# Half-shifted frequencies in a blocked FFT convolution, with shifted filter spectra formed by an add and the taps of the shift convolution summed by accumulating transfers

## The chip, the cores and the metric

The kernel runs on one core of a Trainium2 chip. The metric is the time of one execution on the device in microseconds (us). The core has five engines with a queue of instructions each: PE (TensorE, matrix products into PSUM), DVE (VectorE, elementwise work), ACT (ScalarE, elementwise work and PSUM evictions), POOL (GpSimd, which also issues transfers) and SP (SyncE, which only issues transfers and waits). The engines meet through semaphores.

## The reference

The input is one sequence of S = 2048 rows and D = 640 channels, in bfloat16. Two layers follow each other, each behind a layer norm (LN): a gated long convolution, and a feed-forward network (FFN).

```python
k_shift = sum over t < 4 of k_pad[:, t:t+S, :] * shift_k[:, 3-t]     # 4 taps per channel
kv = k_shift * v
y  = irfft(rfft(kv padded to 2S) * rfft(ssm_k padded to 2S))[:S]      # causal convolution, per channel
y  = y + kv * ssm_D
h  = x + layernorm(x) * y
h2 = h + (silu(layernorm(h) @ w_gate) * (layernorm(h) @ w_up)) @ w_down
```

The FFN's weights are 640 x 1728 (gate, up) and 1728 x 640 (down).

## The kernel before

**Blocks.** The sequence is cut into four blocks of B = 512 rows, j = 0 to 3, and the channels into two halves of CW = 320, c = 0 and 1. The long convolution is computed blockwise. Block i of kv has a spectrum X_i, lag m of the filter has a spectrum K_m, each of a transform of N = 1024 points, and the output of block j is the inverse transform of the sum of X_i K_(j-i). A filter spectrum of lag m covers two neighbouring blocks of the filter, m and m - 1, since a window of 1024 points is needed for an output of 512.

**A transform.** Rows are laid out as four interleaved groups b of 128 rows, so that a transform has two stages with a shuffle between them. In `fwd` (line 704), stage 1 multiplies each group by two 128 x 128 tables; in a K transform of j > 0 it accumulates two sources, the block's filter rows with the table `oS1` and the previous block's with a second table, `oS1A` (line 1100), whose entries carry the sign of the frequency's parity. The result is evicted, and four transfers from SBUF to SBUF regroup the partitions (the shuffle). Stage 2, `stage2` and `spec` (lines 779 and 794), multiplies by 128 x 64 tables, T = 0 and 1 in two halves of PE's columns. h = 0 to 3 numbers the four groups of frequencies, `hs` is a pair of them.

**Frequency 0.** Frequencies are whole numbers, and so 0 and N/2, whose spectra are real, share a row of real and imaginary parts. For that row the product's cross terms differ. K therefore has an extra piece for h = 0 (the cells named "d"): two more matmuls and an eviction of 320 columns in `spec`, four matmuls and an eviction in `dense_h` (line 735), and the second product of h = 0 stands apart from that of the other h (lines 833 to 842).

**Products and inverse.** `products` (line 818) multiplies spectra on DVE: for each term one product of real with real and imaginary with imaginary parts, one of the crossed parts, and adds into two accumulators. `combine` (line 859) forms the real and the imaginary part. For j = 2 the two accumulators aren't combined, and `inv2` (line 869) takes four operands instead of two; for j = 3 the terms of X_1 K_2 and X_2 K_1, summed earlier into the place of X_1, are brought in as two further operands. After `inv2` come an eviction with a scale, a shuffle back (`rs`), and the last stage in `conv_bp` (line 1067), with the gate by the normed x, the residual sum, and the LN's statistics. Block 0 takes a short way: `dense_c` (line 750) multiplies by dense tables of the whole transform, which are loaded at the start in nine pieces (`den_piece`).

**The taps.** `kv_block` (line 976) makes kv: on DVE, a product of the loaded rows of k by each of four taps (t0 and t1 take turns as targets), three adds into t0, and a product with v.

```python
mul(t0, 0); mul(t1, 1); add(); mul(t1, 2); add(); mul(t1, 3); add()
vec(... vt = vt * t0 ...)
```

**Buffers.** Tiles come from pools with few slots, given out in a fixed order. A load into a slot waits until the slot's last reader is done: KIN (rows of k) and VIN (rows of v) have one slot, TMP (t0, t1) two, KT (the filter's rows) three, TX (forward and inverse stages) three, EP (normed rows and gated outputs) four. For most blocks the filter is transposed by a transfer, stored to the scratch tensor `k_nat` and loaded again (`load_kraw`).

**Order.** `Prog.schedule` (line 130) writes every engine's queue out before the kernel runs: it steps through time with a cost for each operation and a model of the transfers (`dma_model`, line 1249), and gives each free engine the ready operation of highest priority. Convolutions go ahead of FFN work, whose matmuls fill the gaps. `pe_end` models the clock of PE. `emit` (line 237) turns the order into instructions with semaphore waits; an instruction whose wait isn't satisfied holds everything behind it on its engine. At the end SP waits for every semaphore that a transfer has used (line 305, `tail`, line 336). Loads for j > 0 and the FFN weights are issued from POOL, the shuffles, the output's stores and the filter's transposes from SP. The `pow` of each LN is also POOL's (line 934).

The functions that the change touches, with the line numbers of the profile:

Of the kernel before, what the change touches and what calls it, by code (L numbers as in the profile page):

```python
# [40 lines left out]
class Prog:  # L41
# [5 lines left out]
    def __init__(self):  # L47
        self.ops, self.pools = [], {}

    def pool(self, name, bases, inorder=False):  # L50
        self.pools[name] = Pool(bases, inorder)

# [55 lines left out]
    def pe_end(self, t, c):  # L108

        w = self.clock  # L110
        while c > 1e-12:
            k = int((t + 1.7) // self.WIN)
# [124 lines left out]
    def emit(self, nc, es, block, ndma_sems):  # L237
# [67 lines left out]
        tail = [(s[0], s[1]) for s in dsem if s[1]]  # L305
# [33 lines left out]
def _tables(R):  # L339
    N = 256 * R  # L340
    B = N // 2
# [3 lines left out]
    s1a = np.zeros((128, 2, 128))  # L345
    for T in range(2):
        f1 = (64 * T + np.arange(64))[None, :]
        s1f[:, T, 0:64] = np.cos(2 * np.pi * q * f1 / 256)
        s1f[:, T, 64:128] = -np.sin(2 * np.pi * q * f1 / 256)
        sg = np.where(f1 % 2 == 0, 1.0, -1.0)  # L350
        s1a[:, T, 0:64] = s1f[:, T, 0:64] * sg
        s1a[:, T, 64:128] = s1f[:, T, 64:128] * sg
    s1f[:, 0, 64] = (-1.0) ** np.arange(128)
    s1a[:, 0, 64] = (-1.0) ** np.arange(128)
    s1i = np.stack([s1f[:, T, :].T for T in range(2)], axis=1)
    w2 = np.zeros((2, R, 128, 2, 64))
    wk = np.zeros((128, 2, 64))
    w2i = np.zeros((128, R, 2, 128))
    for T in range(2):
        for G in range(R):  # L360
            for i in range(I1):
                f1 = 64 * T + R * i + G
                for m in range(R):
                    col = i * R + m
                    for b in range(R):
                        r0, r1 = i * R + b, 64 + i * R + b
                        if f1 == 0:
                            if m == 0:
                                w2[T, G, r0, 0, col] = 1.0
                                w2[T, G, r0, 1, col] = (-1.0) ** b  # L370
                                continue
                            f, r = (256 * m, r0) if m < R // 2 else (128 + 256 * (m - R // 2), r1)
                            th = 2 * np.pi * b * f / N
                            w2[T, G, r, 0, col] = np.cos(th)
                            w2[T, G, r, 1, col] = -np.sin(th)
                            continue
# [7 lines left out]
    wk[:, 0, :] = w2[0, 0, :, 1, :]  # L384
    wk[:, 0, 0] = 0.0
    wk[:, 1, :] = w2[0, 0, :, 0, :]
    wk[:, 1, 0] = w2[0, 0, :, 1, 0]
    w2i[0, 0, :, :] *= 0.5
    w2s = np.transpose(w2, (2, 0, 1, 3, 4)).reshape(128, -1)
    w2in = -w2i[:, :, 0, :]  # L390
    cols = [s1f.reshape(128, -1), s1a.reshape(128, -1), s1i.reshape(128, -1), w2s, wk.reshape(128, -1),
            w2i.reshape(128, -1), w2in.reshape(128, -1), np.eye(128)]
# [7 lines left out]
def _dense_tables(R):  # L400
# [5 lines left out]
    kx = np.zeros((2, R, 128, 128))  # L406
    iv = np.zeros((R, 2, R, 128, 128))
    for h in range(R):
        for T in range(2):
            for i in range(I1):  # L410
                f1 = 64 * T + R * i + h
                for m in range(R):
                    row = T * 64 + i * R + m
                    if f1 == 0 and m == 0:
                        c, s = np.ones_like(t) * 1.0, (-1.0) ** t
                        wc, ws = 0.5 * c, 0.5 * s
                    else:
                        f = f1 + 256 * m
                        if f1 == 0:
                            f = 256 * m if m < R // 2 else 128 + 256 * (m - R // 2)  # L420
                        c = np.cos(2 * np.pi * f * t / N)
                        s = -np.sin(2 * np.pi * f * t / N)
                        wc, ws = c, s
                    fw[h, 0, :, :, row], fw[h, 1, :, :, row] = c, s
                    iv[h, 0, :, row, :], iv[h, 1, :, row, :] = wc, ws
    kx[0], kx[1] = fw[0, 1], fw[0, 0]
    kx[0, :, :, 0] = 0.0
    kx[1, :, :, 0] = fw[0, 1, :, :, 0]
# [4 lines left out]
    return np.concatenate([lay(fw), lay(kx), lay(iv)], axis=1).astype(np.float16)  # L433


def bass_sequential_preLN__ssm_conv_h3__swiglu_ffn__prompt_kernel(
# [12 lines left out]
    CMB = [True, True, False, True]  # L449
    RESPE = [True, True, False, False]  # L450
    KDMA = [[False, False], [True, True], [True, True], [True, True]]
    S2M = False
    I2M = False
# [4 lines left out]
    tab_np, (oS1, oS1A, oS1I, oW2, oWK, oW2I, oW2N, oID) = _tables(R)  # L458
# [8 lines left out]
    with ExitStack() as es:  # L467
        NEL = 101900
# [50 lines left out]
        DROW = fix("drow", D)  # L519
# [5 lines left out]
        HNT = fix("hnt", 5 * 512)  # L525
        WROW = P.tile("wrow", None, HNT.base)
# [7 lines left out]
        P.pool("KT", slots(3, 4 * CW), True)  # L534
# [3 lines left out]
        skb, sk = slots(2, 9 * CW), slots(2, 9 * CW)  # L538
# [9 lines left out]
        P.pool("EK", slots(1, 5 * CW), True)  # L548
        P.pool("PP", slots(3, 4 * CW), True)
        P.pool("P0", [HNT.base + i * 2 * CW for i in range(4)], True)  # L550
        P.pool("EP", slots(4, 2 * CW), True)
# [31 lines left out]
        def dma(subs, kb, reads, writes, prio, eng="sp", after=(), name="", shuffle=False):  # L583
            fns = [(lambda g, d=d, s=s: g.dma_start(d(), s())) for d, s in subs]  # L584
            return P.op({eng: (0.9 if eng == "pool" else 0.5) * len(subs)}, fns, reads, writes, prio, after=after, dma=(kb, shuffle), name=name)
# [39 lines left out]
        def load_kv(j, c, prio):  # L625
# [12 lines left out]
            if j == 0:  # L638
                P.op({"pool": 0.3}, lambda g: g.memset(V(kt, 0, 3 * CW, 0, 1), 0.0), [], [(kt, "z")], prio, name="kz")
# [4 lines left out]
            dma(subs, 573, [], [(kt, 0)], prio, name=f"kin{j}{c}", eng="pool" if j else "sp")  # L644
# [3 lines left out]
        def load_kraw(j, c, prio):  # L648
            if KDMA[j][c]:
# [6 lines left out]
                    [], [(t, 0)], prio, dma=(328 * 3, False), name=f"kraw{j}{c}")  # L656
# [17 lines left out]
        def k_natural(j, c, prio):  # L674
# [18 lines left out]
            pe(fns, 128, 25, [(kr, 0), (IDN, 0)], [(pt, 0)], prio, reserve=[(kt, 0)], name=f"ktr{j}{c}")  # L693
# [10 lines left out]
        def fwd(nm, srcs, pool, prio):  # L704
# [13 lines left out]
            for G in range(R):  # L718
                def src(G=G):
# [3 lines left out]
                    name=f"sh{nm}G{G}", shuffle=True)  # L723
# [5 lines left out]
        def oKX(i, b):  # L729
            return (8 * R + i * R + b) * 128  # L730
# [564 lines left out]
```

## Time and profile before

| | us |
|---|---|
| two executions | 330.1 and 331.59, median 330.85 |
| span of the profiled execution, first to last instruction | 324.5 |
| what the two executions have outside such a span | 5.6 and 7.1 |
| PE busy | 289.4 (89%) |
| DVE busy | 239.2 (74%) |
| ACT busy | 189.7 (58%) |
| POOL busy | 41.6 (13%) |
| transfers | 41.09 MB |

The profile gives the span of the execution that it shows, but not that execution's own time, which is one like the two in the first row. A busy time is the time in which an engine has an instruction in work. The groups of instructions give the mean of one instruction; since instructions overlap in an engine's pipeline, a full stream of them can run faster than the mean tells. Lines are often those of a helper: L593 is any matmul, L816 any operation of two tensors on DVE, L576 any eviction, L584 any transfer.

### The profile page before, as it was taken

The page shows a single profiled execution, that of the slowest core. Times are in us where ns is not written, and L with a number is a line of the kernel's source. Part 1 is how long each engine was busy: PE and PEld are TensorE (multiplying, and loading weights), DVE is VectorE, ACT ScalarE, POOL GpSimd, SP SyncE. Part 2 cuts the span into 40 slices and gives each one's busy share as a digit, 9 for nine tenths or more (in the row PEclk, how much of TensorE's full clock was granted, in tenths as well). Part 3 has the DMA queues.
Part 4 walks back from the last instruction along what each step waited for, and adds up shares of the span by engine and source line. Part 5 has one row for each costly group of instructions (what it writes and reads, how often), then busy time and mean ns, then how long its engine had stood idle before and what let it go on. Part 6 is the DMA issues. An engine that isn't in the chain of part 4 may idle for free. (4 is left out here: it accounts for less than half of the span.)

```text
span 324.5 us, 5040 instructions
## 1 busy us (share of the span) xinstructions
PE 289.4 (89%) x1853; PEld 157.9 (49%) x1872; DVE 239.2 (74%) x416; ACT 189.7 (58%) x304; POOL 41.6 (13%) x55
## 2 busy tenths in 40 slices
PE   4999773589989999998998999789999999999992
PEld 1567451334435466653443566444444576444571
DVE  1988959799899899799999998964598383332221
ACT  4488969767666758577847476679954412222100
POOL 2413125524010003010020000200100010000000
PEclk9999998589999999999999999959999999999999
DMA  7999979879862423424300224241201111000010
GB/s 203 361 403 217 250 232 296 265 210 289 265 194 90 134 103 68 169 91 154 121 2 21 101 63 152 81 154 42 81 0 42 40 41 42 0 2 0 0 53 31
DMA packets 33245, 41.09 MB, mean 127 GB/s; under 512 B 10488, under 2 KB 28307, under 8 KB 33220
## 3 DMA queue, kind: packets, MB, share of 16 engines
q1 hardware_dynamic: 29076, 26.06, 25.8%
q0 software_dynamic: 3296, 14.01, 14.4%
q10 hardware_dynamic: 848, 0.69, 0.8%
q8 instruction: 15, 0.25, 0.3%
q14 instruction: 10, 0.08, 0.1%
HBM read 22.40 MB, written 4.59 MB: 83 GB/s over the span
## 5 line engine op out<-in xcount | busy, mean ns | idle before, releaser
L593 PE MATMUL ps<-sb 128*128 128x320 bf16 (+2 forms) x1193 | 223.6, 339 | 6.4 <-DMA sb<-in_A_shift_k_dram 2.4
L816 DVE TENSOR_TENSOR sb<-sb 128x1280 bf16<-128x1280 bf16 (+2 forms) x266 | 168.8, 677 | 22.6 <-DMA sb<-in_A_k_dram 9.1
L593 PEld LDWEIGHTS ps<-sb 128*128 128x128 bf16 (+2 forms) x1212 | 116.0, 99 | 97.8 <-issue 12.3
L576 ACT ACTIVATE sb<-ps 128x640 bf16<-128x640 f32 (+2 forms) x139 | 94.3, 716 | 39.3 <-PE ps L593 33.5
L816 DVE TENSOR_TENSOR sb<-ps,sb 128x1024 bf16<-128x1024 f32 (+3 forms) x52 | 50.5, 982 | 46.3 <-PE ps L593 42.6
L593 PE MATMUL ps<-sb,tab 128*64 128x320 bf16 (+2 forms) x556 | 69.6, 316 | 13.8 <-ACT sb L576 5.6
L593 PEld LDWEIGHTS ps<-sb,tab 128*64 128x64 f16 (+2 forms) x556 | 34.1, 104 | 49.7 <-issue 21.2
L1165 ACT ACTIVATE sb<-ps 128x1024 bf16<-128x1024 f32 (+2 forms) x32 | 29.3, 915 | 42.1 <-PE ps L593 41.9
L944 ACT ACTIVATE sb<-sb,stt 128x320 bf16<-128x320 bf16 (+1 forms) x43 | 28.7, 722 | 16.5 <-DVE stt L936 12.9
L934 POOL TENSOR_TENSOR stt<-stt 128x2 f32<-128x2 f32 (+1 forms) x12 | 13.8, 1152 | 112.1 <-DVE stt L972 65.3
L579 ACT ACTIVATE sb<-ps 128x640 bf16<-128x640 f32 x24 | 16.0, 702 | 10.5 <-PE ps L593 10.4
L918 DVE BATCH_NORM_STATS2 stt<-sb 128x6 f32<-128x320 bf16 x32 | 13.7, 478 | 0.0
L963 ACT ACTIVATE sb<-sb,stt 128x640 bf16<-128x640 bf16 x16 | 13.2, 827 | 0.3
L1125 PE MATMUL ps<-sb 128*128 128x128 bf16 x80 | 6.8, 249 | 6.4 <-ACT sb L576 3.6
L584 POOL DMA_DIRECT2D sb<-in_A_v_dram x6 | 4.7, 777 | 59.7 <-PE ps L593 56.9
L956 ACT ACTIVATE sb<-sb 128x640 bf16<-128x640 bf16 x16 | 11.9, 742 | 0.0
L1125 PEld LDWEIGHTS ps<-sb 128*128 128x128 bf16 x80 | 5.8, 112 | 7.7 <-ACT sb L576 4.6
L584 POOL DMA_DIRECT2D sb<-in_A_k_dram x6 | 6.0, 995 | 19.7 <-DVE sb L816 19.6
L690 PE MATMUL ps<-sb 128*128 128x128 bf16 (+1 forms) x24 | 4.1, 283 | 2.2 <-DMA sb<-in_A_ssm_k_dram 2.2
L936 DVE TENSOR_TENSOR stt<-stt 128x2 f32<-128x2 f32 (+1 forms) x12 | 1.9, 160 | 5.6 <-POOL stt L934 5.5
L584 POOL DMA_DIRECT2D sb<-in_B_w_down_dram x6 | 4.3, 721 | 11.1 <-DMA sb<-in_B_w_down_dram 7.2
L584 POOL DMA_DIRECT2D sb<-in_B_w_gate_dram x6 | 3.6, 606 | 8.5 <-DMA sb<-in_B_w_gate_dram 7.8
(25 smaller groups left out, 35.3 us busy)
## 6 DMA issues: line engine op xcount, KB each, us to landing
sb<-sb SPq DMA_DIRECT2D x72, 160.0 KB, 2.2
sb<-in_A_k_dram POOLq DMA_DIRECT2D x6, 560.0 KB, 6.5
out_dram<-sb SPq DMA_DIRECT2D x16, 160.0 KB, 1.8
sb<-cst_den SPq DMA_DIRECT2D x9, 256.0 KB, 5.8
sb<-in_B_w_gate_dram POOLq DMA_DIRECT2D x5, 416.0 KB, 5.4
sb<-in_B_w_up_dram POOLq DMA_DIRECT2D x5, 416.0 KB, 6.0
sb<-in_A_q_dram POOLq DMA_DIRECT2D x3, 640.0 KB, 5.5
sb<-in_A_v_dram POOLq DMA_DIRECT2D x6, 320.0 KB, 4.4
```

The source lines that it names most:

```text
L576: fns = {"act": lambda a: a.activation(out=dst(), in_=src(), func=ACTF.Copy), "dve": lambda v: v.tensor_copy(out=dst(), in_=src())}
L579: fns = {"act": lambda a: a.activation(out=dst(), in_=src(), func=ACTF.Copy, scale=scale), "dve": lambda v: v.tensor_scalar(out=dst(), in0 ...
L584: fns = [(lambda g, d=d, s=s: g.dma_start(d(), s())) for d, s in subs]
L593: return lambda t: t.matmul(o(), l(), r(), start=st, stop=sp)
L816: return lambda v: v.tensor_tensor(out=o(), in0=a(), in1=b_(), op=op)
L918: vec(dve1(CW, False), lambda v: v.bn_stats(st6(l, j, b, c), V(xt, b * D + c * CW, CW)), [(xt, (b, c))], [(ST, ("s", l, j, b, c))], prio, ...
L934: P.op({"pool": 0.4}, lambda g: g.tensor_tensor(out=y, in0=va, in1=stt[:, 420:420 + hi - lo], op=ALU.pow), c1 + [(ST, "half")], c3, prio, ...
L944: "act": lambda a: a.activation(out=dst(), in_=src(), func=ACTF.Identity, scale=rs(l, j, b), bias=tmv(l, j, 3)[:, b:b + 1])},
L956: P.op({"act": act_c(D) + 0.22}, lambda a, b=b, jt=jt: a.activation(out=V(jt, 0, D), in_=V(xt, b * D, D), func=ACTF.Copy, accum_out=tmv(l, ...
L963: P.op({"act": act_c(D) + 0.3}, lambda a, b=b, jt=jt: a.activation(out=V(jt, 0, D), in_=V(xt, b * D, D), func=ACTF.Square, bias=tmv(l, j, ...
L1125: fns.append(lambda t, k=k, d=d: t.transpose(B16(pt, k, d * 128, 128), V(hn[k], d * 128, 128), V(IDN, 0, 128)))
L1165: P.op({"act": act_c(n)}, lambda a: a.activation(out=dst(), in_=src(), func=ACTF.Silu), rd, wr, -1000, name=f"si{j}{i}")
```

## The change

1. **Odd frequencies.** All frequencies are shifted by a half: f1 becomes f1 + 0.5 in all tables. No spectrum is real then, and the extra piece for frequency 0, its tables, matmuls, evictions and the split product go. The tables get smaller: the dense ones from 9 x 1024 to 8 x 1024 columns, the small one from 3584 to 2688.
2. **Shifted spectra by an add.** Stage 1 of K takes one source only. The spectrum of the block's own filter rows goes to a new tile SS (a pool of five slots), and `shift_add` makes the filter spectrum of the lag from it and the previous block's: two DVE operations of 640 elements per partition for each pair of h. KT falls to two slots.
3. **Two operands in every inverse.** For j = 2 the accumulators are combined too, and for j = 3 the earlier sums are added on DVE (`cx`, two operations for each pair of h) instead of in `inv2`.
4. **Tap sums by transfers.** For j > 0 the three adds of `kv_block` become three transfers from SBUF to SBUF that add to t0, issued from POOL. The product with the fourth tap is written over the k rows.
5. **Smaller things.** The gated output takes the place of the normed tile (EP falls to three slots). At the end SP waits for the semaphores of the output's last stores only. DROW lies in GUT. The costs and the model of transfers in the scheduler change, and with them the order that it writes.

```diff
-        tail = [(s[0], s[1]) for s in dsem if s[1]]
+        last = {}
+        for o in self.ops:
+            if o.dma is not None and not o.succ and o.name.startswith("st"):
+                last[id(o.sem)] = (o.sem, max(o.semval, last.get(id(o.sem), (None, 0))[1]))
+        tail = list(last.values())
...
-        f1 = (64 * T + np.arange(64))[None, :]
+        f1 = (64 * T + np.arange(64))[None, :] + 0.5
...
-    return np.concatenate([lay(fw), lay(kx), lay(iv)], axis=1).astype(np.float16)
+    return np.concatenate([lay(fw), lay(iv)], axis=1).astype(np.float16)
...
-        P.pool("KT", slots(3, 4 * CW), True)
+        P.pool("KT", slots(2, 4 * CW), True)
...
+        P.pool("SS", slots(5, 4 * CW), True)
...
-        P.pool("EP", slots(4, 2 * CW), True)
+        P.pool("EP", slots(3, 2 * CW), True)
...
+        def shift_add(dst, do, cur_, co, prv, po, hs, prio, nm):
+            rd = [(t, h) for t in (cur_, prv) for h in hs]
+            wr = [(dst, h) for h in hs]
+            o1 = vec(dve2(640), tt(lambda: V2(dst, do, 960, 2, CW), lambda: V2(cur_, co, 960, 2, CW), lambda: V2(prv, po + CW, CW, 2, CW), ALU.subtract),
+                     rd, [(dst, (h, "a")) for h in hs], prio, name=f"ks{nm}")
+            vec(dve2(640), tt(lambda: V2(dst, do + CW, CW, 2, CW), lambda: V2(cur_, co + CW, CW, 2, CW), lambda: V2(prv, po, 960, 2, CW), ALU.add),
+                rd + [(dst, (h, "a")) for h in hs], wr, prio, name=f"kp{nm}")
...
+            def acc(src, off, cells):
+                P.op({"pool": 1.0}, [lambda g: g.dma_start(V(t0, 0, W4), V(src, off, W4), accum_op=ALU.add)],
+                     [(t0, 0)] + cells, [(t0, 0)], prio, dma=(656, "acc"), name=f"kvd{j}{c}")
+
             mul(t0, 0)
             mul(t1, 1)
...
+            else:
+                acc(t1, 0, [(t1, 0)])
+                mul(t1, 2)
+                vec(dve2(W4), tt(lambda: v4(kt), lambda: v4(kt), lambda: tapb(3), ALU.mult),
+                    [(kt, 0), (kt, "z"), (TAPS, 3)], [(kt, 0)], prio, name=f"kvm{j}{c}")
+                acc(kt, 0, [(kt, 0)])
+                acc(t1, 0, [(t1, 0)])
...
-            if CMB[j]:
+            if j < 3:
                 combine(...)
+            else:
+                ax = SXt[1, c]
+                combine(...)
+                for a, o_ in ((a1, 0), (a2, CW)):
+                    vec(dve2(640), tt(lambda a=a: V2(a, 0, 640, n, CW), lambda a=a: V2(a, 0, 640, n, CW), lambda o_=o_: V2(ax, h0 * 640 + o_, 640, n, CW), ALU.add), ...,
+                        name=f"cx{nm}{h0}")
...
-            srcs = [(kts[j, c], oS1)] + ([(kts[j - 1, c], oS1A)] if j else [])
-            uk = fwd(f"K{j}{c}", srcs, "TK", pb + 104)
+            uk = fwd(f"K{j}{c}", [(kts[j, c], oS1)], "TK", pb + 104)
...
-            for hs in ([[0], [1], [2], [3]] if j == 0 else [[0, 1], [2, 3]]):
+            for hs in ([0, 1], [2, 3]):
...
-        link = [1.4]
+        link, turn = [2.6], [0.0]
...
-                    [], [(t, 0)], prio, dma=(328 * 3, False), name=f"kraw{j}{c}")
+                    [], [(t, 0)], prio, dma=(328, "turn"), name=f"kraw{j}{c}")
...
+            if kind == "shuffle":
+                s = max(issued, dmafree[0])
+                dmafree[0] = s + 0.3
+                return s + 1.65 + (1.6 if link[0] > issued else 0.0)
+            if kind == "store":
+                return issued + 1.3
+            if kind == "turn":
+                s = max(issued, link[0] + 1.0 if link[0] > issued + 2.0 else 0.0, turn[0])
+                turn[0] = s + 4.9
+                return turn[0]
+            s = max(issued + (1.3 if o.eng == "pool" else 0.9), link[0])
+            link[0] = s + kb / 345.0
+            return link[0] + 1.0
```

## The prediction, made before the change was run

> **What bounds it now.** First the page's first and second parts, for who is busy and when.
>
> ```profile
> span 324.5 us, 5040 instructions
> ...
> PE 289.4 (89%) x1853; PEld 157.9 (49%) x1872; DVE 239.2 (74%) x416; ACT 189.7 (58%) x304; POOL 41.6 (13%) x55
> ...
> PE   4999773589989999998998999789999999999992
> ...
> DVE  1988959799899899799999998964598383332221
> ...
> PEclk9999998589999999999999999959999999999999
> DMA  7999979879862423424300224241201111000010
> ```
>
> PE is the fullest, but DVE stands at 9 until slice 26. So I cut the span where its character changes: the table of windows (stretch, length; busy us of PE, PEld, DVE, ACT, POOL; clock; DMA share; GB/s).
>
> ```profile
> 52.00:58.00 6.00, 2.07 (x14) 0.86 (x14) 4.69 (x16) 6.00 (x12) 5.05 (x5) 0.65 1.07 335
> ...
> 64.00:124.00 60.00, 56.71 (x343) 27.13 (x348) 56.00 (x91) 41.23 (x62) 7.95 (x11) 0.97 0.59 178
> 124.00:182.00 58.00, 54.45 (x358) 28.31 (x360) 54.20 (x86) 40.22 (x65) 6.13 (x6) 1.00 0.27 90
> 182.00:207.00 25.00, 24.90 (x198) 16.34 (x200) 23.69 (x46) 13.87 (x23) 1.52 (x2) 1.00 0.28 99
> ...
> 213.00:268.00 55.00, 54.24 (x339) 27.91 (x344) 36.89 (x67) 32.64 (x56) 2.44 (x3) 0.96 0.14 53
> ```
>
> To 64 us transfers and short dependences leave PE idle; 64 to 207 has PE and DVE both at 93 to 100%; from 213 PE alone is full. Next, the groups by shape, for prices (count | busy us, mean ns | idle).
>
> ```profile
> L816 DVE TENSOR_TENSOR sb<-sb 128x1280 bf16<-128x1280 bf16 x158 | 127.2, 826 | 17.6 <-DMA sb<-in_A_k_dram 9.1 <-PE ps L593 4.1 <-DMA sb<-in_A_v_dram 1.8
> ...
> L816 DVE TENSOR_TENSOR sb<-sb 128x640 bf16<-128x640 bf16 x92 | 42.2, 483 | 5.0 <-PE ps L593 3.1 <-ACT sb L576 1.3
> ...
> L593 PE MATMUL ps<-sb,tab 128*128 128x320 bf16 x192 | 32.6, 299 | 5.4 <-DMA sb<-k_nat 3.1 <-ACT sb L576 2.2
> ...
> L593 PE MATMUL ps<-sb,tab 64*128 64x320 bf16 x160 | 14.5, 315 | 3.1 <-DVE sb L816 3.1
> ```
>
> Last the chain of waits (start, length, what), one row of the timeline, the tail line's row, and the landing of the output tensor's stores:
>
> ```profile
> 182.10 25.20 PE ps L593 x198
> ...
> 269.50 3.80 PE ps L593 x28
> ...
> 302.83 15.40 PE ps L593 x112
> ```
> ```profile
> 42.13 1.26 PE L593 MATMUL ps<-sb,tab 128*128 128x320 bf16 x8 [3.08 <-DMA sb<-k_nat]
> ```
> ```profile
> L336 SPq EVENT_SEMAPHORE  x69: 17/28/28, 319.6 to 324.1; - x69
> ```
> ```profile
> DMA to landing us min/median/max: 1.8/1.8/5.6
> ```
>
> The third piece gives 15.40/112 = 0.1375 us per 320-column matmul in a full stream; the timeline row shows PE standing 3.08 us for one transfer; the tail row shows 69 final waits, the last at 324.1.
>
> **The change, part by part.**
>
> *PE.* Stage 1 of K loses its second source: 8 matmuls in each of 6 blocks (j = 1 to 3, c = 0, 1), 48 x 0.1375 = 6.6 us. `inv2` goes from four operands to two for j = 2 and 3: 64 of the 160 half-height matmuls, which run two at a time, 32 x 0.1375 = 4.4. The extra spectrum of frequency 0 goes: 8 dense matmuls, 1.1, and 12 half-width ones in pairs, 0.8. Together 12.9 us of 289.4. ACT also loses 8 evictions of 320 columns (437 ns each); ACT isn't the limit.
>
> *DVE.* Gone: 18 adds of 1280 (three in each of six blocks), 18 x 0.826 = 14.9. Eighteen pairs of 640 products become one of 1280: 18 x (2 x 0.483 - 0.826) = 2.5. New, all 640: 24 in `shift_add`, 8 in `combine` for j = 2, 8 `cx` for j = 3: 40 x 0.483 = 19.3. Net +1.9 us. But it moves: in 64 to 207, 24 new (11.6), against 15 adds (12.4) and 14 merges (2.0): -2.8.
>
> *Tail.* SP waits only for the semaphores of the last stores, at most 16. The last store is issued at 319.2 and lands 1.8 later, at 321.0; the end at 324.1 is the list of waits, paid in full. Gain 3.0; bounds 2.5 (sixteen waits of 28 ns may follow the landing) and 3.1.
>
> *Start.* The dense tables shrink from nine pieces of 256 KB to eight, the small table from 896 to 672 KB: 480 KB, at the 282 to 372 GB/s of 10 to 30 us 1.3 to 1.7 us of a link whose share is 1. The dense stage loses 1.1 us of PE. The transfer models change too, so the order does: now PE waits 3.1 us at 39 to 42 for `k_nat` in front of dense work that was ready. The new model gives the transpose 4.9 us, which may move that stage-1 matmul back. Bounds 0 and 1.7 + 3.1 = 4.8; I take 3.1, about two thirds, since the link and this stall are in the chain to the first FFN at 64.
>
> *64 to 207.* PE sheds 8 x 0.1375 for each of K11, K20, K21, K30 (4.4), 2.2 in `inv2` of j = 2, 0.6 in the frequency-0 matmuls: 7.2. DVE sheds 2.8. Where both are full the smaller cut decides; the last 25.2 us, by the chain, are PE's own. So 2.0 (most of DVE's 2.8, up to 182) + 2.0 (PE's share after it: K31 or K30, half an `inv2`) = 4.0; bounds 0 and 7.2. The EP pool falls from four slots to three, so in the LN wait at 207 the fourth normalised tile waits for a transpose of 0.7 us: 0.7 back; bounds 0 and 0.7 at each of four LNs, 2.8.
>
> *207 to the end.* Of j = 3's PE work 2.2 (K stage 1) + 2.2 + 0.3 = 4.7 goes. What covers j = 3's convolution is FFN 2; its LN transposes run at 268.2 with one `dn` of 28 matmuls, 3.8 us, left in reserve. The cover shrinks by 4.7, the chain grows by four 640 operations, 4 x 0.45 = 1.8: 4.7 + 1.8 - 3.8 = 2.7 idle. Gain 2.0; bounds 0 and 4.7.
>
> *The accumulating transfers.* 18 of 320 KB, SBUF to SBUF, from POOL's queue: no row shows one. Issue: the 560 KB loads from there took 0.95 to 1.1 us, the 320 KB ones 0.78; I take 1.0, 18 us on a POOL 13% busy. Landing: from below 2.2 (160 KB shuffles), from above 8.8, twice the 4.4 of the 320 KB `A_v` loads on that queue, as the target is read too; I take 4.4, the row of equal size, queue and row length. Three in series are 3 x 5.4 = 16.2 us, where three adds took 2.5. This I cost at nothing, as most tap sums wait anyway: `vin` of (2,1), (3,0), (3,1) is issued 34, 54 and 61 us after its `kin`. That cover is thin for (1,0), (1,1) and (2,0): 9, 10 and 19 us. What they delay, by some 7 us (16.2 less 9 or 10), is a K or X stage 1, under which FFN 0 (64 to 140) runs; LN of j = 1 came 8 us before `dn` 0 ran out. What stands behind the waits: on DVE, the second product into t1 waits for the first transfer to have read it, and `kvv` for the third; every later DVE instruction is queued behind. On POOL, weight pieces, loads and the LN `pow` are. KIN is held until the second transfer lands, so the next `kin` is later too. KT goes from three slots to two, but no block reads the previous K any more, so `kld` on SP finds its slot as early as now; SS is new and its slots come free at the next j's `shift_add`, ahead of need. A gain from them beyond the adds I exclude. Bounds 0 to +23, below.
>
> POOL's own row in 60 to 200 us, beside a DVE 93% busy, shows that its issues aren't starved:
>
> ```profile
> L584 POOL DMA_DIRECT2D sb<-in_B_w_down_dram x6 | 4.3, 721 | 11.1 <-DMA sb<-in_B_w_down_dram 7.2 <-DMA sb<-in_B_w_up_dram 3.8
> L584 POOL DMA_DIRECT2D sb<-in_A_k_dram x4 | 3.9, 979 | 13.9 <-DVE sb L816 13.9
> ```
>
> Against the change speaks the Trainium skill, SBUF — State Buffer, section "Who interferes with whom": GpSimd writes the descriptors of its own queue, shares a port pair with DVE, and some DVE instructions lock it out. By the example in that page's section "A bandwidth-pool intuition that's wrong", where such a transfer grew from about 0.62 to 3.1 us, each accumulation would come 2.5 us later, and with one DVE wait in each of five blocks the total would be +12, about 332. The sum goes by the row.
>
> **Sum.** -3.0 -3.1 -4.0 +0.7 -2.0 = -11.4: span 313.1. Outside the span lie 5.6 to 7.1 us in the two runs (330.1, 331.59), 6.35 at the median: 319.5. Best bounds, 3.1 + 4.8 + 7.2 + 4.7 = 19.8, give 311. Forecast's own range 312 to 324.
>
> **Rivals.**
>
> A, *PE counts alone*: DVE has enough holes, and all 12.9 come through with the tail 3.0 and 2.0 of the stall: 330.85 - 17.9 = 313. For: after 182 the chain is all PE. Against: DVE's 93% before that.
>
> B, *the cut is hidden*: both streams wait on convolution latency, since four buffers for (j,c) share three TX slots, and longer tap sums and `shift_add` eat the freed PE time, so the change does not do what it says. The tail remains: 327.9. For: the LN waits at 58 and 207. Against: FFN work covers most of the rest.
>
> C, *slower: DVE stands at the transfers*. The order is fixed beforehand, and assumes a landing 4.2 us after issue. If one takes 8.8, DVE waits 4.6 us at the t1 product in five blocks after 64, uncovered because DVE is 93% busy: +23, 342. It decides from an excess of 11.4/5 = 2.3 us, landing at 6.5, which is what the 560 KB loads took. For: DVE already waits 3.4 us for `A_k` loads in 64 to 207. Against: tap products are low in priority and are placed late.
>
> **Chances.** Forecast 0.62, A 0.15, B 0.14, C 0.09. Two per cent, about what a measurement of this kernel can tell from no change, is 324.2 to 337.5: faster 0.77 (forecast and A), same 0.14 (B), slower 0.09 (C). The range goes down to 309, 2 under the best bound and A, for an order that also shortens the LN waits, and up to 329, B with 1 more, leaving out C and some of the ends.
>
> **What would show it.** Last wait within 0.5 us of the last landing; PE near 276.5 busy, stage-1 128*128 count 144, 64*128 count 96; 1280 products 158 - 18 + 18 = 158, 640 ones 92 + 40 - 36 = 96; no `k_nat` wait; transfers from sb to sb on POOL landing near 4.4. Wrong if they land above 6.5 with DVE idle behind them, if LN of j = 2 comes later than 207, or if PE in 64 to 207 falls under 90%.

## The result, and the profile after

The changed kernel takes 340.9 us (two runs, 340.3 and 341.4) against 330.85 before: the ratio is 1.0325, with a 95% interval of 1.0249 to 1.0401. I had forecast 319.5, with a range that ended at 329. Slower by 10 us, then, where 11 us of gain were expected. Below, kernels are compared by their ratio to the kernel before on the same chip (328.9 to 329.2 us there; 0.01 is 3.3 us). The medians are over all runs, the ratios leave out disturbed ones, so the two can differ by some tenths of a per cent.

The spans have grown by more than the times, from 324.5 to 338.5 us. In every execution for which both figures are on record, those of the kernel before included, 1.8 to 1.9 us lie outside the span. So the profiled execution of before took about 326.3 us, less than either of the two that were timed, and the 5.6 and 7.1 us of the table of before compare different executions.

The page of the profiled execution (340.3 us, of which 1.8 lie outside the span), its first three parts in the lines that answer to those shown of before:

```profile
span 338.5 us, 4739 instructions
...
PE 284.5 (84%) x1724; PEld 151.8 (45%) x1740; DVE 242.1 (72%) x427; ACT 183.2 (54%) x289; POOL 55.1 (16%) x73
...
PE   4999735897999999189999995347999999999996
...
DVE  1967974517796988879999899996889856222311
...
PEclk9999985697999999759999998575999999999999
DMA  7999979899589866540233524651030111000011
...
q0 software_dynamic: 5888, 19.91, 24.4%
```

DVE, which stood at 7 to 9 in slices 7 to 12, now shows 4 5 1 7 7 9 there (51 to 102 us). The DMA engines had fallen to 2 and 4 in slices 13 and 14, and now stay at 9 and 8. PE has holes around 140 us and from 203 to 237, and the granted clock falls with them. POOL's queue (q0) moved 14.01 MB before in 14.4% of the time of 16 engines.

The stretches are the same as before (length; busy us of PE, PEld, DVE, ACT, POOL; clock; DMA share; GB/s):

```profile
64.00:124.00 60.00, 55.35 (x328) 26.45 (x331) 40.70 (x59) 37.58 (x55) 11.73 (x14) 0.96 0.89 221
124.00:182.00 58.00, 47.92 (x290) 24.37 (x292) 53.81 (x94) 38.15 (x63) 9.33 (x11) 0.91 0.39 112
182.00:207.00 25.00, 24.24 (x171) 15.39 (x169) 23.55 (x35) 11.77 (x18) 4.33 (x5) 1.00 0.37 99
213.00:268.00 55.00, 42.54 (x239) 18.85 (x242) 46.87 (x89) 36.45 (x59) 4.83 (x5) 0.82 0.27 84
```

The first row has the loss: DVE did 40.7 us of work in 64 to 124 where it had done 56.0, and the DMA share is 0.89 where it was 0.59. The next row shows PE short of work for it. The LN transposes on PE give the same picture as dates. The first of each LN starts at 59.1 (j = 0), 127.3, 209.5 and 268.2 us before, and at 55.9, 143.3, 227.0 and 285.3 after. So the start comes 3 us earlier, 19 us are lost under FFN 0, and the delay of 16 to 17.5 us is carried to the end.

Where DVE stands, in the timeline of DVE and then of POOL (start, length, what, idle before and its releaser):

```profile
69.24 1.23 DVE L756 TENSOR_TENSOR sb<-ps,sb 128x1024 bf16<-128x1024 f32 x1 [5.07 <-PE ps L559]
76.65 1.69 DVE L756 TENSOR_TENSOR sb<-sb 128x1280 bf16<-128x1280 bf16 x2 [6.18 <-DMA sb<-sb]
```
```profile
64.48 0.93 POOL L932 DMA_DIRECT2D sb<-sb  x1 [0.48 <-DVE sb L756]
65.48 0.77 POOL L550 DMA_DIRECT2D sb<-in_B_w_down_dram  x1
75.42 0.72 POOL L550 DMA_DIRECT2D sb<-in_B_w_down_dram  x1 [9.17 <-DMA sb<-in_B_w_down_dram]
76.14 0.77 POOL L550 DMA_DIRECT2D sb<-in_A_v_dram  x1
78.36 0.70 POOL L550 DMA_DIRECT2D sb<-in_B_w_down_dram  x1 [1.46 <-DMA sb<-in_B_w_down_dram]
79.07 0.97 POOL L932 DMA_DIRECT2D sb<-sb  x1
...
86.96 0.99 POOL L550 DMA_DIRECT2D sb<-in_A_k_dram  x1 [4.85 <-DMA sb<-sb]
87.93 0.96 POOL L932 DMA_DIRECT2D sb<-sb  x1
```

These are the three accumulations of one tap sum, (1,1). The first is issued at 64.48 and lands 12.1 us later, when DVE at 76.65 may overwrite t1. The second needs the two products that DVE makes then, done at 78.34; it stands on POOL behind a piece of `w_down` that is issued at 78.36, so the queue costs it 0.7 us at most. The load of the next block's k, at 86.96, waits for the second landing, and the third accumulation stands behind that load. The sum takes from 64.48 to 93.7, 29 us, where I had counted 16.2. Here it is the landings that make the difference: 25.1 us in sum, where I had 13.2. The chain of waits runs through these rows (start, length, what):

```profile
65.48 12.60 DMA sb<-in_B_w_down_dram
...
79.07 7.32 DMA sb<-sb
...
87.93 5.75 DMA sb<-sb
```

In the sum before it, (1,0), POOL's queue shows itself:

```profile
44.56 0.91 POOL L932 DMA_DIRECT2D sb<-sb  x1 [5.57 <-DVE stt L892]
48.77 0.95 POOL L550 DMA_DIRECT2D sb<-in_A_k_dram  x1 [2.19 <-DMA sb<-sb]
...
53.83 0.95 POOL L932 DMA_DIRECT2D sb<-sb  x1
```

The second accumulation lands 3.6 us after its issue, at 48.2, and the product that the third one adds is older than that. But the third is issued 5.7 us later, behind the load of k, two `pow` and two pieces of `w_up`.

All 18 transfers together, in the row of their line (shortest, median and longest time from issue to landing):

```profile
DMA to landing us min/median/max: 3.5/4.4/12.1
```

### The profile page after: what moved, and what is told of

Its sections match the earlier page's. It is cut to its first block, busy times and chain, and to the rows that moved or that the text cites. A ratio compares the mean times of both kernels' runs of the same rounds, so it can differ in the third digit from the quotient of the medians.

```text
span 338.5 us, 4739 instructions
## 1 busy us (share of the span) xinstructions
PE 284.5 (84%) x1724; PEld 151.8 (45%) x1740; DVE 242.1 (72%) x427; ACT 183.2 (54%) x289; POOL 55.1 (16%) x73
## 3 DMA queue, kind: packets, MB, share of 16 engines
q0 software_dynamic: 5888, 19.91, 24.4%
## 4 chain that ended last, share of the span: by engine, by line
PE 50%; DVE 21%; DMA 15%; ACT 7%; issue 4%; POOL 1%; ACTq 0%; DVEq 0%; POOLq 0%
PE ps L559 49%; DVE sb L756 18%; DMA sb<-sb 9%; DMA sb<-in_B_w_down_dram 4%; ACT sb L542 3%; ACT sb L877 3%; DMA sb<-in_A_ssm_k_dram 2%; DMA out_dram<-sb 1%; DVE stt L851 1%; ACT sb L545 1%; DVE sb L876 1%; ACT sb L1115 1%; PE ps L1075 1%; PE ps L656 1%; ACT sb L896 1%
## 5 line engine op out<-in xcount | busy, mean ns | idle before, releaser
L756 DVE TENSOR_TENSOR sb<-sb 128x1280 bf16<-128x1280 bf16 (+1 forms) x270 | 169.5, 675 | 35.0 <-ACT sb L542 11.2
L542 ACT ACTIVATE sb<-ps 128x640 bf16<-128x640 f32 (+1 forms) x131 | 90.4, 729 | 51.4 <-PE ps L559 45.0
L559 PE MATMUL ps<-sb,tab 128*64 128x320 bf16 (+2 forms) x432 | 61.0, 336 | 24.9 <-DMA sb<-sb 15.2
L559 PEld LDWEIGHTS ps<-sb,tab 128*64 128x64 f16 (+2 forms) x432 | 26.2, 108 | 58.9 <-issue 22.9
L877 ACT ACTIVATE sb<-sb,stt 128x320 bf16<-128x320 bf16 (+1 forms) x36 | 24.9, 730 | 17.5 <-DVE stt L869 16.7
L932 POOL DMA_DIRECT2D sb<-sb x18 | 16.2, 902 | 67.2 <-issue 18.7
L867 POOL TENSOR_TENSOR stt<-stt 128x2 f32<-128x2 f32 (+1 forms) x12 | 11.4, 953 | 62.8 <-DVE stt L905 49.6
L1075 PE MATMUL ps<-sb 128*128 128x128 bf16 x80 | 8.9, 287 | 14.5 <-ACT sb L877 7.6
L1075 PEld LDWEIGHTS ps<-sb 128*128 128x128 bf16 x80 | 7.2, 131 | 17.5 <-ACT sb L877 13.0
L896 ACT ACTIVATE sb<-sb,stt 128x640 bf16<-128x640 bf16 x16 | 13.2, 826 | 1.3 <-DVE stt L892 1.2
L550 POOL DMA_DIRECT2D sb<-in_B_w_down_dram x6 | 4.3, 724 | 14.1 <-DMA sb<-in_B_w_down_dram 12.1
L876 DVE TENSOR_SCALAR sb<-sb,stt 128x320 bf16<-128x320 bf16 (+1 forms) x12 | 5.0, 439 | 0.4 <-PE ps L1075 0.3
```

What stands on the lines that cost most here:

```text
L542: fns = {"act": lambda a: a.activation(out=dst(), in_=src(), func=ACTF.Copy), "dve": lambda v: v.tensor_copy(out=dst(), in_=src())}
L559: return lambda t: t.matmul(o(), l(), r(), start=st, stop=sp)
L756: return lambda v: v.tensor_tensor(out=o(), in0=a(), in1=b_(), op=op)
L877: "act": lambda a: a.activation(out=dst(), in_=src(), func=ACTF.Identity, scale=rs(l, j, b), bias=tmv(l, j, 3)[:, b:b + 1])},
L896: P.op({"act": act_c(D) + 0.3}, lambda a, b=b, jt=jt: a.activation(out=V(jt, 0, D), in_=V(xt, b * D, D), func=ACTF.Square, bias=tmv(l, j, ...
L932: P.op({"pool": 1.0}, [lambda g: g.dma_start(V(t0, 0, W4), V(src, off, W4), accum_op=ALU.add)], [(t0, 0)] + cells, [(t0, 0)], prio, dma=(6 ...
```

## The experiments

My theory after the result was that the accumulating transfers cost all of the loss. That can happen in three ways: by their bytes on DMA engines that are full until about 100 us (L), by POOL's queue, in which loads stand behind waiting accumulations and the reverse (P), or by the series of products and landings with the one k slot held through two of them (S). The rivals were that the new transforms or the new order cost. Each edit gets a new order from the kernel's planner, so a comparison holds a change of order too, except where it is said that the order is the same.

**1. All sums on DVE.** The changed kernel without its transfers, and three runs beside it:

```diff
-            if j == 0:        # kv_block: adds on DVE for j = 0 alone
+            if True:          # e1_adds
+            if j < 2:         # e2_acc_from_j2
```

> The changed kernel with the three adds of each tap sum back on DVE in all blocks; all else as changed. Theory (the accumulating transfers put the tap sums of blocks (1,0) and (1,1) on the path: the LN transposes of j = 1 came at 143 to 147 us against 127 to 129 before, those of j = 2 at 227 to 231 against 209): transposes of j = 1 back to 125 to 131, of j = 2 to 207 to 214, time 323 to 330, although DVE is 14.9 us busier. Rival 1 (the extra spectrum work on DVE, 40 operations, is the cost): no faster than the changed kernel, 340 or more. Rival 2 (the new order and its transfer model are the cost): 335 to 342.

Measured: 325.4 us, ratio 0.9872 (0.9823 to 0.992). As expected. Against 1.0325 the transfers cost 4.5%, 15 us, and everything else in the change is worth -1.3%. LN of j = 1 and 2 come at 128.6 and 212.5 us, as the theory asked.

> The changed kernel with accumulating transfers only for j = 2 and 3, adds on DVE for j = 0 and 1. Theory: the loss lies in j = 1, where the link is full and the load of v follows 10 us after that of k, so this comes within 3 us of the kernel with adds everywhere, or under it since DVE is 9.9 us less busy: 320 to 328. Rival (each of the waits costs something wherever it stands): about a third of the way back only for each j, 330 to 336.

Measured: 338.4 us, 1.0218 (1.0133 to 1.0302). This is a miss: I had thought that only the thin cover of j = 1 cost, and the sums of j = 2 and 3 carry most of it.

The transfers alone, put into the kernel before (the same `acc` and the same branch for j > 0 in its `kv_block`):

> The kernel before with the accumulating transfers for j = 1 to 3 as its one edit (modelled like loads of 656 KB). Theory: slower by 10 to 20 us, 341 to 351, with the LN transposes of j = 1 at 137 to 147 us. Rival (transfers are harmless by themselves, the spectra or the order cost): 325 to 333.

Measured: 349.3 us, 1.0443 (1.0344 to 1.0542). As expected. They cost 4.4% there too, so it isn't the company of the new transforms that makes them dear.

> The kernel before with the shorter list of final waits as its one edit. Theory: span shorter by 3.0 us (2.5 to 3.1), time 327.8. Rival (the last semaphores are waited for elsewhere, or the end of the program has its own cost that hides them): within 1 us of before.

The edit is the list of final waits of the changed kernel in the kernel before. Measured: 331.3 us, but over 325.0 to 339.9, so the times decide nothing. The trace does: from the end of DVE's last instruction to the end of the span it is 2.3 us (327.43 to 329.7), where it was 5.35 before (319.15 to 324.5).

**2. Tail.** To see it in the time, the shorter list was taken out of `e1_adds`:

```diff
-        tail = list(last.values())
+        tail = [(s[0], s[1]) for s in dsem if s[1]]
```

> e1_adds (325.4 us) with SP's final waits as before the change: for every semaphore of a transfer instead of the last stores alone. If the tail is worth what the prediction took for it: 328.4, the last DVE operation 5.3 us ahead of the end instead of 2.3. If the end was hidden behind the store anyway: 325.4, within 1.

Measured: 328.75 us, 0.9998 (0.9955 to 1.0041). In the two timelines, DVE's last instruction and the spans (325.5 here, 323.4 in `e1_adds`):

```profile
319.29 0.82 DVE L756 TENSOR_TENSOR sb<-ps,sb 128x640 bf16<-128x640 f32 x1 [2.98 <-PE ps L559]
```
```profile
320.31 0.83 DVE L756 TENSOR_TENSOR sb<-ps,sb 128x640 bf16<-128x640 f32 x1 [2.98 <-PE ps L559]
```

From the end of that instruction to the end of the span it is 5.4 us with the old list and 2.3 with the new one. The tail gives 3.1 us, and without it and the transfers nothing is left of the change: 0.9998.

**3. Which sums.** The last of the three additions of each tap sum as a transfer, so that the k slot isn't held; then all three, but for j = 3 alone; then for (2,1) and j = 3. The lines are against `e1_adds`:

```diff
                 mul(t1, 3)
-                add()
+                acc(t1, 0, [(t1, 0)])          # e6_last_acc, j > 0
-            if True:
+            if j < 3:                          # e7_acc_j3
+            if (j, c) < (2, 1):                # e11_acc_from_21
```

> e1_adds (325.4 us), but for j of 1 to 3 the last of the three additions is an accumulating transfer, 6 in all; the fourth product goes to the second temporary, so DVE frees the k slot as with adds. Six DVE adds (5 us) are gone, one landing (3.5 to 8 us) stands ahead of each v product. If the cost goes by the number of landings in series (18 cost 14.5 us), a third of it: 329 to 332. If it is the k slot, held until the second landing, that costs: 322 to 327.

Measured: 334.3 us, 1.0147 (1.0065 to 1.023), 2.75% over `e1_adds`. That is above both values. Six transfers, with the k slot free, cost 9 us: it takes no held slot to make them dear.

> e1_adds (325.4 us), but the six additions of j = 3 are accumulating transfers as in the changed kernel (its k slot is held too). Accumulating from j = 2 on cost 13 us over e1_adds and shifted LN of j = 1 by 3, of j = 2 by 12 us. If the sums of j = 2 carried that (their k slots came late, and DVE idled while it should have worked ahead), j = 3 alone is covered: 322 to 328. If the sums of j = 3 carried it (they stand behind stores and x loads on POOL before LN of j = 2), 331 to 338.

Measured: 324.1 us, 0.9858 (0.9789 to 0.9927), the best of all kernels here, though not to be told from `e1_adds`. Transfers that start between 114 and 170 us cost nothing. Their landings are short:

```profile
DMA to landing us min/median/max: 3.5/3.6/5.9
```

> The version with accumulating transfers for j = 3 alone (324.1 us) with those of the second half of j = 2 added, 9 transfers in all. They would be issued after some 100 us, where the engines of the link are half idle in that version's trace (0.5 to 0.6 of 16 engines). Theory L: no cost, and three DVE adds (2.5 us) fewer while DVE is busy 19 of 20 us: 321 to 325. If the j = 2 sums cost because they come early in the series for LN of j = 2, whatever the link does: 328 to 336.

Measured: 330.1 us, 1.0015 (0.9961 to 1.0069): 1.6% over the version with j = 3 alone, so theory L by itself failed here (though the first of the three is issued at 92.8 us, in a stretch with a share of 0.84, and not after 100). POOL's rows show what the three early transfers pushed back. First the load of k for (3,1) in `e7_acc_j3`, then in this kernel:

```profile
128.82 0.99 POOL L550 DMA_DIRECT2D sb<-in_A_k_dram  x1 [3.34 <-DMA sb<-sb]
```
```profile
147.41 0.98 POOL L550 DMA_DIRECT2D sb<-in_A_k_dram  x1 [3.80 <-DMA sb<-sb]
...
192.06 0.90 POOL L932 DMA_DIRECT2D sb<-sb  x1
197.08 0.56 POOL L550 DMA_DIRECT2D sb<-in_A_q_dram  x1 [4.12 <-DMA out_dram<-sb]
197.63 0.89 POOL L932 DMA_DIRECT2D sb<-sb  x1
```

That load is 18.6 us later, and the last accumulation stands behind an x load that waits for a store. LN of j = 2 came at 214.2 instead of 208.5 us.

**4. Bytes against waits.** Transfers that nobody reads, 18 of them, added to `e1_adds`:

```diff
+            def ghost(n):                      # after each product of j > 0; m is that product
+                i = 6 * (j - 1) + 3 * c + n
+                prev[:] = [P.op({"pool": 1.0}, [lambda g: g.dma_start(g_dram.ap()[i * 128:(i + 1) * 128], V(TAPS, 0, 4 * D))],
+                                [(TAPS, k) for k in range(4)], [], prio, after=[m] + prev, dma=(656, "acc"), name=f"kvd{j}{c}")]
```

> The kernel with all tap sums added on DVE (e1_adds, 325.4 us), plus 18 transfers that nobody waits for: at each place where the changed kernel has an accumulating transfer, POOL issues a plain one of 655 KB from the tap rows in SBUF to an unused DRAM scratch (twice 320 KB, because an accumulated MB was seen to keep the DMA engines twice as long as a loaded one), after the same DVE product and after the landing of the one before it. Nothing of the computation is left out. Link, POOL queue and POOL's waits are then as in the changed kernel; what is missing is that DVE and the k and v slots wait for the landings. Theory S (the series: DVE's products, the k slot and the v product stand behind three landings each): within 3 us of e1_adds, 323 to 328.5. Theory Q (queue and link: the transfers fill the 16 engines and keep POOL's loads and powers waiting, whoever reads the sums): most of the 14.5 us stays, 334 to 341.

Measured: 347.0 us, 1.0465 (1.0346 to 1.0584). Nobody waits for a landing but POOL's next issue, and the loss is no smaller than the changed kernel's and over theory Q's range, so S isn't needed for it. (These transfers went to DRAM. By the row of POOL's queue, 22.8% of 345.9 us against 13.7% of 323.4 in `e1_adds`, they kept 16 engines busy for 34.6 us; the 18 accumulations of the changed kernel took 38.3.) The same with an eighth of the bytes (`V(TAPS, 0, CW)`), in the same order on every engine:

> e5_ghost (347.0 us) with each unread transfer cut from 128 rows of 2560 elements to 128 rows of 320, an eighth of the bytes (82 KB); the order of the instructions on every engine, the 18 issues on POOL and what POOL waits for stay as they were. Theory L (the bytes: the extra transfers lengthen every load and shuffle of a link that is full until about 100 us): the cost goes with them, 324 to 330. Theory P (the order: POOL stands at the products and landings with its loads and powers behind it, and the engines' orders were made for that): most of it stays, 338 to 346.

Measured: 332.0 us, 1.0135 (1.0056 to 1.0214), between the two theories. By the ratios, 3.3% go with the bytes, and 2.6% over `e1_adds` stay; the planned order and POOL's waits are not separated in them. And the changed kernel itself, with the accumulations over 128 of their 1280 columns, in the same order:

```diff
-                P.op({"pool": 1.0}, [lambda g: g.dma_start(V(t0, 0, W4), V(src, off, W4), accum_op=ALU.add)],
+                P.op({"pool": 1.0}, [lambda g: g.dma_start(V(t0, 0, 128), V(src, off, 128), accum_op=ALU.add)],
```

> The changed kernel (340.9 us) with each of its 18 accumulating transfers over 128 of the 1280 columns; the other columns of the tap sums are left out. Every wait, the order of the instructions and the held k slots stay; a tenth of the bytes moves. Theory L (bytes on a full link): 325 to 331. Theory S (the series of product, issue, landing, product that holds the k slot and the v product; a small landing still takes some 2 us of the 4.4): about half of the 14.5 us stays, 332 to 336. Theory P (POOL's order): 337 to 341.

Measured: 335.3 us, 1.0206 (1.0115 to 1.0297): the value of theory S, but nothing in it tells S from P. Only 1.2% (4 us) went with the bytes here, and the two intervals overlap.

**5. POOL's queue.** The 15 loads of k, v and x for j > 0 go to SP, in the changed kernel, in `e1_adds`, and in the narrow version:

```diff
-            dma(subs, 760, [], [(kt, 0)], prio, name=f"kin{j}{c}", eng="pool" if j else "sp")
+            dma(subs, 760, [], [(kt, 0)], prio, name=f"kin{j}{c}", eng="sp")
...                                             # the same for vin and x
```

> The changed kernel (340.9 us) with the loads of k, v and x for j of 1 to 3 (15 transfers) issued by SP instead of POOL, so that on POOL only the pieces of the weights, the powers and the accumulations share a queue. Nothing is left out. Of the 14.5 us that the accumulations cost over e1_adds, the narrow transfers took off 5.6; about 10 stay. Theory P (the queue: accumulations stand behind waiting loads and loads behind waiting accumulations): most of the 10 goes, 330 to 334. Theory S (the series: product, issue, landing, product, with one k slot held through two landings, whichever queue loads it): 337 to 343.

Measured: 342.3 us, 1.049 (1.0337 to 1.0644). By the number, theory S; but see the narrow version.

> e1_adds (325.4 us) with the same 15 loads on SP: the control for the run before it, all sums on DVE. POOL's queue holds up nothing here by the trace (its waits are for slots), while SP then has a wait for a slot ahead of shuffles: 323 to 330 by either theory. If it gains as much as the run before it, the gain has nothing to do with the accumulations.

Measured: 329.0 us, 1.0102 (0.9959 to 1.0245), the control. It is 2.3% above `e1_adds`: the move of the loads, with its new order, may cost something by itself, but the interval is wide.

> Both together: the loads of k, v and x on SP, and each accumulating transfer over 128 of 1280 columns (the other columns of the tap sums are left out). Bytes and POOL's queue are then out, the series of products and (shorter) landings stays. Theory P: all of the cost gone, 323 to 328. Theory S: 331 to 336, about where the narrow transfers alone ended (335.3).

Measured: 327.0 us, 1.0016 (0.996 to 1.0073). So the series of products and landings, k slot held and all, costs nothing against that control once the landings are short and the loads are out of POOL's way. Theory S, which asked for 331 to 336, fails. The ratios in one table:

| sums of j > 0 | k, v, x loads on POOL | k, v, x loads on SP |
|---|---|---|
| DVE adds | 0.987 | 1.010 |
| accumulated, 128 columns | 1.021 | 1.002 |
| accumulated, 1280 columns | 1.0325 | 1.049 |

The first row is the control of each column. With the loads on POOL the narrow sums still cost 3.3% over it. With the loads on SP the wide ones still cost 3.9%, and the narrow ones nothing (0.8% less than the control, within the intervals). Against `e1_adds` that last kernel is still 1.4% slower, so the cost is gone only if the move of the loads is what costs the rest. From the second row to the third the order is the same, and the right-hand step of 4.7% (16 us) is bytes and landing time alone. The step from left to right in the second row, 1.9% (6 us), is POOL's queue and the new order together, which no run separates; in the other two rows the ratio goes up with the same move. In the waits of the narrow version on SP, POOL stands before its accumulations for about as long as in the wide one, 82.9 us (us in total, times, longest), and no load of k, v or x is behind it:

```profile
POOL sb L932 <- DVE sb L756: 85.7, 9, 17.5
```

What the bytes do can be read off two kernels with one order, the two with the loads on SP. In the timeline of PE, the first stage-2 matmuls of two shuffles, wide and then narrow; the first pair waits alike, the second 8.56 and 1.63 us:

```profile
50.02 0.46 PE L559 MATMUL ps<-sb,tab 128*64 128x320 bf16 x4 [4.73 <-DMA sb<-sb]
59.04 1.28 PE L559 MATMUL ps<-sb,tab 128*64 128x320 bf16 x8 [8.56 <-DMA sb<-sb]
```
```profile
50.85 0.75 PE L559 MATMUL ps<-sb,tab 128*64 128x320 bf16 x4 [4.93 <-DMA sb<-sb]
53.22 1.28 PE L559 MATMUL ps<-sb,tab 128*64 128x320 bf16 x8 [1.63 <-DMA sb<-sb]
```

and the windows from 40 us on, wide and then narrow (columns as above):

```profile
40.00:60.00 20.00, 5.84 (x42) 3.40 (x42) 9.72 (x32) 8.62 (x17) 8.38 (x13) 0.76 0.95 259
...
80.00:100.00 20.00, 14.74 (x74) 6.02 (x72) 11.69 (x18) 8.11 (x12) 1.49 (x2) 0.83 0.91 198
```
```profile
40.00:60.00 20.00, 10.19 (x67) 5.80 (x68) 15.43 (x43) 14.01 (x24) 8.53 (x12) 0.70 0.78 240
...
80.00:100.00 20.00, 19.63 (x122) 9.38 (x123) 18.29 (x29) 14.62 (x22) 1.72 (x2) 1.00 0.62 177
```

The wide transfers keep the engines' share at 0.91 to 0.95 in windows where it is 0.78 and 0.62 with the narrow ones. What pays here is not the reader of the sum but the shuffle of a transform that happens to share the engines: it lands late, PE waits for it, and DVE has 9.72 us of work in 40 to 60 instead of 15.43.

Two things stay open. A wide transfer both fills the engines and lands later, and no run separates these two inside the changed kernel; the sum (1,1) above shows the long landings at work there. And of the 3.3% that the narrow transfers cost on POOL, it isn't shown how much is the queue and how much the order that was planned for the transfers.

## Why the prediction was wrong, step by step

**Accumulating transfers: the step that failed.** "This I cost at nothing, as most tap sums wait anyway." The price of one was right: issue 0.83 to 0.97 us (1.0 taken), median landing 4.4 (4.4 taken), nothing starved. Three things were wrong around it. The series of a sum is 18 to 35 us, not 16.2, and 29 to 30 in the two sums of j = 1, since the second and third transfer wait for the landing before them, for a DVE product and for what stands ahead of them on POOL. The bound of 8.8 us was too low: in the busy stage one landed after 12.1. And I asked only who waits for the transfers, and didn't ask whom their bytes delay, although the page of before has the DMA row at 7 to 9 up to slice 10; where that could be measured with one order it was 4.7% with the loads on SP, and 1.2%, not clear of the noise, in the changed kernel's own order. POOL's queue I did name ("weight pieces, loads and the LN `pow` are" behind the waits), and put no price on it. The term was 0 with bounds of 0 to +23; it measured 15.

**64 to 207 us: -4.0 predicted, a loss instead.** "Where both are full the smaller cut decides" was the right rule, but DVE's cut of 2.8 was there only because 12.4 us of adds had left it. With the adds back on DVE (`e1_adds`), its window shows what becomes of PE's cut; in 182 to 207 PE had been busy for 24.90 us and DVE for 23.69:

```profile
182.00:207.00 25.00, 13.92 (x94) 7.09 (x90) 23.68 (x36) 13.80 (x25) 1.34 (x2) 0.73 0.30 105
```

PE's FFN work ends at 189 us instead of 207, and from 191.3 PE waits 6.3 us for DVE; DVE is as full as before, and LN of j = 2 comes at 212.5 us (209.5 before). PE's 25.2 us from 182 on in the chain were the work at hand, not the limit. One part of the working was off without effect: the 2.2 us of K's stage 1 after 207 are two blocks, but of the six, K10 runs ahead of 64 us and four are in the list for 64 to 207, so that one is left. It enters the cover and the work alike, and the 2.0 for the end stays as it is.

**PE -12.9.** The counts came as said: 144 full-height matmuls (stage 1 and the last stage), 96 of `inv2`, and of DVE's operations 158 and 96:

```profile
L756 DVE TENSOR_TENSOR sb<-sb 128x1280 bf16<-128x1280 bf16 x158 | 126.6, 826 | 23.7 <-DMA sb<-sb 11.2 <-DMA sb<-in_A_k_dram 6.0 <-PE ps L559 4.6
...
L756 DVE TENSOR_TENSOR sb<-sb 128x640 bf16<-128x640 bf16 x96 | 45.0, 486 | 11.2 <-ACT sb L542 10.5
...
L559 PE MATMUL ps<-sb,tab 128*128 128x320 bf16 x144 | 27.9, 318 | 7.9 <-DMA sb<-sb 5.5 <-ACT sb L542 1.7 <-DVE sb L756 0.6
...
L559 PE MATMUL ps<-sb,tab 64*128 64x320 bf16 x96 | 10.7, 339 | 4.9 <-DVE sb L756 4.2 <-ACT sb L542 0.7
```

But PE was busy for 284.5 us, not 276.5: 8.0 of the 12.9 us don't show. The matmuls of these rows took longer, 318 ns in the mean instead of 299 and 339 instead of 315, while the other 320-column ones stayed at 304. The mean granted clock fell from 0.967 to 0.919. That the rest went into slower or more scattered matmuls is argued from this, not shown by a run. (`e1_adds`, with 285.1 us, tells less: its trace has 540 matmuls of 512 columns, where that of before has 521 and the changed kernel's 524 for the same FFN, so records are missing in those.)

**Tail -3.0.** Right: 3.1 by the timelines, and the last store, issued at 336.2, lands 1.8 later, 0.5 ahead of the end. **Start -3.1.** The stall for `k_nat` is gone, and LN of j = 0 comes 3.2 us earlier, though only 1.0 in `e1_adds`. **207 to the end, -2.0.** From the first LN transpose of j = 2 to that of j = 3 it took 58.7 us before and 58.3 after, so -0.4. **DVE +1.9** was +2.9 (239.2 to 242.1). **Outside the span.** The 6.35 us measured 1.8, since it was worked out from two different executions. The 0.7 for the EP slots can't be seen by itself.

**Rivals.** C gave 342 for 340.9, but that was luck in the main: it came by another way. It wanted a landing above 6.5 us in general and 23 us of DVE at the transfers. Three of 18 landed later than that, and the waits list has DVE behind transfers for half as much:

```profile
DVE sb L756 <- DMA sb<-sb: 11.2, 5, 6.2
```

Of its counter-argument, that tap products are placed late, e7 shows the true half (j = 3) and e2 the false one. B, the cut hidden and the tail kept, is nearly what `e1_adds` is: 0.991 by its 327.9, 0.987 measured. Two of the signs that I had set against myself, "if LN of j = 2 comes later than 207, or if PE in 64 to 207 falls under 90%", came true: its first transpose is at 227.0 (209.5 before, so the mark of 207 was itself early), and PE is busy for 127.5 of 143 us, 89%. The third, landings above 6.5 us with DVE idle behind them, came true for one transfer, the one of 12.1 us.

## What to carry to other kernels

In these runs a transfer that replaced an engine's work had three prices, not one: the landing for its reader, its place in a queue for what stands behind it, and its bytes for all others on the DMA engines. Read the DMA row of the profile at the time when it will run; six transfers cost nothing where the share was 0.3 to 0.6 (j = 3), and six cost 9 us where the first three ran at 0.74 to 0.95 (the last of each sum). And when two engines are full, take work from the one that sets the next wait; here the cut on the other one, PE, became idle time, at a granted clock of 0.73 in 182 to 207 us of `e1_adds` where it had been 1.00.

## What the runs showed of the hardware

- An accumulated megabyte keeps the DMA engines busy twice as long as a loaded one. From `e1_adds` to the changed kernel, POOL's queue grew by 5.90 MB and from 13.7% of 323.4 us to 24.4% of 338.5: 38.3 us for 5.90 MB, 6.5 us a MB, where the loads alone took 44.3 us for 14.01 MB, 3.2 a MB. What the loads lose beside them is within the 6.5. The same working gives 5.9 to 8.3 in the other runs with fewer of these transfers or in the kernel before (`e2_acc_from_j2`, `e3_before_acc`, `e6_last_acc`, `e7_acc_j3`, `e11_acc_from_21`).
- One accumulation of 320 KB from SBUF to SBUF lands 3.5 to 5.9 us after issue when the engines are about half idle or more (`e7_acc_j3`, shares of 0.29 to 0.57 from 100 to 180 us), and up to 12.1 after it when they are full (the changed kernel, 0.89 from 64 to 124). Over 128 columns, a tenth of it, the shortest landing is 2.1 us against 3.5, and the longest in the changed kernel's order still 9.4. The 18 narrow ones kept the engines busy for 10.3 us (16.3% of 334.9 less the same 44.3), about a quarter of what the wide ones took.
- POOL's issue of them took 834 to 966 ns, by the stretches above beside a DVE busy for 68 to 94% of the time from 64 to 207 us. The lock-out of POOL's descriptor writing by DVE, of which the Trainium skill, SBUF — State Buffer, section "Who interferes with whom", warns, isn't seen in these runs. That agrees with the section, which names `copy`, `cast` and `tensor_scalar` for it and says that `tensor_tensor` didn't stall transfers; `tensor_tensor` is 219.9 of DVE's 242.1 us here. The prediction's 332 by that page left this out.
- The granted clock of PE was 0.967 on average in the profile before (0.94 to 0.97 over its other executions), and 0.91 to 0.94 in every version with the new transforms, even in those that were faster.
